# Norm 1's squares as diagonal blocks on TensorE, a far table laid out by lag column, and wider fillers, in a fused S4-and-MLP kernel

## The chip, the cores and the metric

The kernel runs on one core of one Trainium2 chip. The metric is the device time of one execution in microseconds (us), the median of several runs. A run is called slow when it lies over 1.5% above the fastest run of the same kernel; every comparison below is of fast runs unless it says otherwise. Within a trace, times count from the first instruction; the time of a run is about 1.7 us over its span.

TensorE is called PE in the views, its weight loads PEld, VectorE DVE, ScalarE ACT, GpSimd POOL; SP issues transfers. When this text speaks of a *row*, it means one instruction in TensorE's own stream: a weight load and its matmul are two rows, and a bare wait of its sequencer is one.

## The reference, cut to what matters

```python
def reference(A_u, ..., B_w1, B_b1, B_w2, B_b2):      # u: 2048 tokens x 512 channels
    # A: layernorm -> S4 convolution along the tokens (kernel K from A, B, C, dt) -> + u*Dskip
    K = jnp.einsum("dn,dnl,dn->dl", Cc, P, dB).real
    y = irfft(rfft(u_padded) * rfft(K_padded))[:L]
    h = x + A_ref(layernorm(x), ...)
    # B: layernorm -> MLP that mixes TOKENS: 2048 -> 1792 -> gelu -> 2048
    u = jnp.einsum("bsd,sf->bdf", layernorm(h), w1) + b1
    y = jnp.einsum("bdf,fs->bds", gelu(u), w2) + b2
    return h + y.transpose(0, 2, 1)
```

The kernel does the convolution in two ranges. Near lags go through small transforms of 128-token chunks; far lags through 32x32 *lag tiles* (`lag`) that multiply a *far table* G with the windowed means of earlier chunks, Mb. The first half of the chunks has its lag tiles early, the second half later.

## The kernel before: the parts that the change and the argument touch

Statistics of norm 1, on VectorE and ScalarE, two halves of eight 128-token chunks:

```python
def ln1(self, hf):
    for k in range(lo, hi):
        if k < hi - na:
            b.bn(self.st1[:, k, :], self.X[:, k, :])                       # VectorE, 512 wide
        else:                                                             # ScalarE, two passes
            b.act(self.junk[:, :], self.X[:, k], AF.Copy, accum_out=self.s1[:, 0, k:k + 1])
            b.act(self.cb[:, 0], self.X[:, k], AF.Square, accum_out=self.s1[:, 1, k:k + 1])
    ...                          # scales Fs, window weights WL, mean correction mb (PSUM bank 3)
def moments(self, hf):
    ...                          # ms = WL^T X + mb, in PSUM bank 3, copied out by ScalarE
def shifted(self, hf):
    # ms goes to HBM and comes back shifted, as Mb
```

The far table and the lag tiles:

```python
GB = (4, 2, 6)                    # first PSUM bank of each pair
def far(self):
    for i in range(0, NJ, 2):
        bb = GB[(i // 2) % len(GB)]
        for q in range(2):
            b.mm(self.bank(bb + q), self.tb("wi", (i + q) * P, P)[rows], self.kt[rows], pack=2)   # 512 columns
        ...                       # 1024-wide copies into G[p, x, i, s]
def lag(self, hf):
    for s in ...:
        for q in range(4):
            b.mm(self.ps[32*q:32*q+32, 32*s:32*s+32], Gv[:, q, s], Mv[:, q, s])   # 32x32 result tiles
```

The order of instructions on each engine isn't written by hand: a list scheduler in the program makes it at build time from priorities, dependencies and estimated costs. And it puts *fillers*, useless matmuls, where it expects TensorE to be idle.

```python
    self.near_kernel(); self.far(); self.lag(0)
    self.ln1(1); self.moments(1); self.shifted(1); self.spectrum(1)
    self.lag(1); self.rest(); self.mlp2()
    r.schedule(); r.emit_all()
```

## Time and profile before

| what | us |
|---|---|
| time, median of 3 runs (156.23 to 156.44) | 156.26 |
| span of the profiled run | 154.7 |
| big kernel table T complete | 35.17 |
| kt (short-lag values that the far table is made from) out of PSUM | 39.69 |
| first residual add, y0 | 50.11 |
| TensorE without gaps from | 57.45 |
| last addition starts | 152.34 |

Read it as a relay: tables on VectorE until 35, samples and far table until 45, lag tiles and convolution output until 57, and from there TensorE alone sets the end. The lines are in the prediction.

Two lines that the prediction did not show matter below: one of the waits (engine, line, what was waited for: us in total, times, longest), and one of the transfer queues, where *instruction* is the queue that brings instructions to the core (transfers, MB, share):

```profile
PE ps L499 <- issue: 0.4, 2, 0.2
```

```profile
q8 instruction: 12, 0.20, 0.5%
```

"issue" is idle time for which the profile shows no cause.

### The profile page before, as it was taken

How to read it: one execution, taken by the hardware profiler on the slowest of the kernel's cores; microseconds unless marked ns; L12 is line 12 of the kernel's file. 1: busy time of each engine (PE TensorE's matmuls, PEld its weight loads, DVE VectorE, ACT ScalarE, POOL GpSimd, SP SyncE). 2: the span in 40 equal slices, each digit the busy share in tenths (PEclk: the TensorE clock that was granted, in tenths of full speed). 3: DMA queues.
4: the chain of work that ended last, by engine and by line, in shares of the span. 5: the costliest groups of instructions: out<-in, count | busy, mean ns of one | idle time of the engine just before them, and what ended most of it. 6: DMA issues, size and time to landing. Idle time of an engine off the chain costs nothing.

```text
span 154.7 us, 3685 instructions
## 1 busy us (share of the span) xinstructions
PE 143.5 (93%) x1522; PEld 106.7 (69%) x1529; DVE 131.4 (85%) x308; ACT 78.2 (51%) x192; POOL 6.7 (4%) x11
## 2 busy tenths in 40 slices
PE   7849869989998889999999999999999999999993
PEld 3738753568565485545554788888888888888882
DVE  5099999998999998999999999957999994558663
ACT  4897999998997868614544832545320000000000
POOL 1590000000000000000000000000000000000000
PEclk9999999999999999999999999999999999999999
DMA  4899996266992508995590000000000101211123
GB/s 108 264 310 360 406 403 240 65 230 176 417 372 83 202 4 310 419 408 222 166 375 3 0 6 0 0 0 4 0 0 0 38 34 68 71 54 51 66 73 103
DMA packets 12351, 23.64 MB, mean 153 GB/s; under 512 B 1181, under 2 KB 8350, under 8 KB 12206
## 3 DMA queue, kind: packets, MB, share of 16 engines
q1 hardware_dynamic: 12190, 23.27, 41.8%
q8 instruction: 12, 0.20, 0.5%
q10 hardware_dynamic: 144, 0.13, 0.2%
q14 instruction: 5, 0.04, 0.1%
HBM read 21.17 MB, written 2.35 MB: 152 GB/s over the span
## 4 chain that ended last, share of the span: by engine, by line
PE 67%; DMA 14%; DVE 7%; SPq 5%; ACT 3%; issue 2%
PE ps L499 67%; DMA tab<-tables 8%; SPq L556 5%; DMA Mb<-ms_scratch 4%; DVE T L522 3%; DVE cmu L522 3%; DMA ms_scratch<-ms 2%; ACT G L506 1%; DVE ct L522 1%; ACT UF L506 1%; PE ps L784 1%; ACT ms L506 0%; ACT kf L506 0%; DVE X L536 0%; ACT mb L506 0%
## 5 line engine op out<-in xcount | busy, mean ns | idle before, releaser
L499 PE MATMUL ps<-H,W 128*128 128x512 bf16 (+1 forms) x180 | 32.5, 327 | 0.3 <-issue 0.2
L499 PEld LDWEIGHTS ps<-H,W 128*128 128x128 bf16 x184 | 17.7, 98 | 10.6 <-DVE H L532 0.2
L784 PE MATMUL ps<-idf 128*128 128x256 bf16 x162 | 22.0, 282 | 1.0 <-POOL idf L547 1.0
L499 PE MATMUL ps<-gT,W 128*128 128x256 bf16 x182 | 22.6, 273 | 0.0
L499 PEld LDWEIGHTS ps<-gT,W 128*128 128x128 bf16 x182 | 17.0, 98 | 3.0 <-DVE X L522 0.2
L784 PEld LDWEIGHTS ps<-idf 128*128 128x128 bf16 x162 | 15.6, 101 | 4.3 <-POOL idf L547 1.0
L522 DVE TENSOR_TENSOR W<-W 128x1024 bf16<-128x1024 bf16 (+1 forms) x23 | 14.9, 657 | 0.3 <-PE ps L499 0.2
L522 DVE TENSOR_TENSOR X<-ps,acc 128x256 bf16<-128x256 f32 x24 | 10.0, 422 | 5.5 <-PE ps L499 5.2
L499 PE MATMUL ps<-HT,W 128*128 128x256 bf16 x112 | 14.2, 273 | 0.0
L506 ACT ACTIVATE H<-X 128x512 bf16<-128x512 bf16 x16 | 10.0, 624 | 7.7 <-DVE X L536 7.7
L536 DVE SCALAR_TENSOR_TENSOR acc<-ps,b2T,X 128x256 f32<-128x256 f32 x24 | 11.1, 481 | 2.8 <-PE ps L499 2.2
L499 PEld LDWEIGHTS ps<-HT,W 128*128 128x128 bf16 x112 | 10.9, 98 | 1.4
L499 PE MATMUL ps<-TS,S 128*128 128x256 bf16 x84 | 11.6, 273 | 0.0
L499 PE MATMUL ps<-TS,W 128*128 128x256 bf16 x84 | 11.3, 273 | 0.0
L536 DVE SCALAR_TENSOR_TENSOR X<-ps,X 128x512 bf16<-128x512 f32 x16 | 10.6, 687 | 0.2 <-PE ps L499 0.2
L506 ACT ACTIVATE gT<-snap,b1T 128x256 bf16<-128x256 f32 x12 | 6.0, 505 | 9.1 <-DVE snap L522 9.1
L542 DVE BATCH_NORM_STATS2 st<-X 128x6 f32<-128x512 bf16 x12 | 7.4, 679 | 3.5 <-DMA X<-in_A_u_dram 3.5
L506 ACT ACTIVATE UF<-ps,ub 128x512 bf16<-128x512 f32 x16 | 10.2, 686 | 0.2 <-PE ps L499 0.2
L499 PEld LDWEIGHTS ps<-TS,S 128*128 128x128 bf16 x84 | 7.9, 98 | 1.4 <-DVE acc L536 0.4
L499 PEld LDWEIGHTS ps<-TS,W 128*128 128x128 bf16 x84 | 8.2, 98 | 1.0
L506 ACT ACTIVATE gT<-ps,b1T 128x512 bf16<-128x512 f32 (+1 forms) x10 | 5.4, 606 | 4.7 <-PE ps L499 4.7
L499 PEld LDWEIGHTS ps<-O,tab 128*128 128x128 bf16 x64 | 4.8, 98 | 3.9 <-DVE O L530 0.8
(127 smaller groups left out, 233.4 us busy)
## 6 DMA issues: line engine op xcount, KB each, us to landing
W<-in_B_w_dram SPq DMA_DIRECT2D x4, 1792.0 KB, 10.9
W<-in_B_w_dram SPq DMA_DIRECT2D x2, 2048.0 KB, 9.3
W<-in_B_w_dram SPq DMA_DIRECT2D x2, 1536.0 KB, 7.9
Mb<-ms_scratch SPq DMA_DIRECT2D x2, 1024.0 KB, 6.0
out_dram<-X SPq DMA_DIRECT2D x15, 128.0 KB, 1.7
tab<-tables SPq DMA_DIRECT2D x1, 1296.0 KB, 13.1
X<-in_A_u_dram SPq DMA_DIRECT2D x4, 256.0 KB, 4.7
X<-in_A_u_dram SPq DMA_DIRECT2D x2, 512.0 KB, 11.8
```

Of the source, the lines that this page charges most:

```text
L499: return self.r.add("pe", lambda e: e.matmul(out, lhsT=lhsT, rhs=rhs, start=start, stop=stop, skip_group_check=onto), [lhsT, rhs], [out], ...
L506: return self.r.add("act", lambda e: e.activation(out=out, in_=in_, func=func, bias=bias, scale=scale, accum_out=accum_out), [in_, bias, s ...
L522: return self.r.add(eng, lambda e: e.tensor_tensor(out=out, in0=a, in1=b, op=op), [a, b], [out], self._d(eng, nel(out), m), **k)
L536: return self.r.add(eng, lambda e: e.scalar_tensor_tensor(out=out, in0=a, scalar=s, in1=b, op0=op0, op1=op1, accum_out=accum_out), [a, s, ...
L542: return self.r.add("dve", lambda e: e.bn_stats(out=out, in_=a), [a], [out], 67 + nel(a) / 0.96, **k)
L556: return self.r.add(eng, lambda e: e.dma_start(out=out, in_=in_), [in_], [out], max(by / RATE.get(out.tensor.name.split("_")[0], 410) + 0. ...
L784: self.rec.hot = (hot, lambda e, bk: e.matmul(self.bank(bk, 0, 256), lhsT=hv[:, 0:P], rhs=hv[:, :], start=True, stop=True))
```

## The change

The intent: take norm 1's statistics off the crowded VectorE and ScalarE. X is loaded a second time, transposed, and TensorE squares it as 64-token diagonal blocks. The far table is made in blocks of four lag columns, so that the first lag tiles can start when half of it is copied, and is stored so that a tile's weight columns lie next to each other. The scheduler now counts lag tiles as four side by side (`slow` and `pack` change its cost estimates, not the instructions). One more pair of column blocks of MLP 1 uses the product with seven multiplications instead of eight. Fillers are 512 columns instead of 256 and start at 20.5 us instead of 8. The core of it, with cuts:

```diff
-GB = (4, 2, 6)
+GB = (4, 2, 6, 4)
-WARM = (8000.0, 48000.0)
+WARM = (27000.0, 48000.0)
+HOT = 20500.0
@@ loads
+        for h in range(2):
+            ld(17 + h, self.XT[:, h], self.x_in[0][L // 2 * h:L // 2 * h + L // 2], transpose=True)
+            ld(8 + h, self.X[:, 8 * h:8 * h + 8], xv[:, 8 * h:8 * h + 8])
@@ statistics (all of them before moments(0))
-                b.bn(self.st1[:, k, :], self.X[:, k, :])
+    def stats(self, hf):
+        for k in range(8):
+            for c in range(4):
+                for q in range(2):
+                    t = XT[:, c, P * k + 64 * q:P * k + 64 * q + 64]
+                    b.mm(self.bank(bk, 64*k, 64*k+64, 64*q, 64*q+64), t, t, start=c == 0, stop=c == 3, onto=True, pack=2)
+        ...   # 32 column sums per half; diagonal by a masked product and a reduction on VectorE
@@ far: 64 columns at a time, one lag column each
-                b.mm(self.bank(bb + q), self.tb("wi", (i + q) * P, P)[rows], self.kt[rows], pack=2)
+            for i in range(NJ):
+                for q in range(2):
+                    b.mm(self.bank(bb + q, 64*i, 64*i+64), self.tb("wi", i * P, P)[rows], kt[rows, c + q], pack=2)
@@ lag
-                    b.mm(self.ps[...], Gv[:, q, s], Mv[:, q, s])
+                    b.mm(self.ps[...], Gv[:, h, q, s - 16 * h], Mv[:, q, s], slow=8.5, pack=4)
@@ W1: two quarters before the tables and two after -> one after the first means, three after the second
-        for q in range(2):
-            ld(13 + q, self.W1[...], w1v[...])
+        self.w1q(*((1, 2, 3) if hf else (0,)))
@@ MLP 1: four pairs of column blocks -> five; fillers 256 -> 512 columns
```

## The prediction

> **What bounds the kernel now**

> I read the chain of waits first, then the busy table cut at the points where that chain changes engine, then the timelines of the five engines, and last the groups by shape. The chain, in order of time (start us, length us, what):

> ```profile
> 33.72 0.05 issue
> 33.76 3.49 PE ps L499 x126
> ...
> 40.21 1.94 ACT G L506 x2
> ...
> 44.22 0.70 ACT ms L506
> 44.91 0.02 issue
> 44.93 3.14 DMA ms_scratch<-ms
> 48.07 0.02 issue
> 48.09 6.31 DMA Mb<-ms_scratch
> 54.40 0.04 issue
> 54.44 2.85 PE ps L499 x114
> ...
> 81.83 70.49 PE ps L499 x621
> 152.32 0.03 issue
> 152.34 0.48 DVE X L536
> ```

> Up to 33.7 the chain is the VectorE making the kernel tables. Then TensorE samples them (x126), ScalarE copies the far table G, and the chain goes over to the second half of norm 1: its moments ms leave only at 44.2, go out to HBM and come back as Mb at 54.4. The second half of the lag products (x114 of 128) waits for that. From 57.4 on TensorE never stops. The busy time of each engine in those stretches (columns: PE, PEld, DVE, ACT, POOL, clock, DMA share, GB/s):

> ```profile
> 34.00:44.00 10.00, 9.72 (x225) 7.03 (x221) 9.26 (x21) 9.32 (x25) 0.00 (x0) 1.00 0.78 288
> 44.00:50.10 6.10, 5.42 (x144) 3.91 (x145) 5.82 (x9) 4.94 (x11) 0.00 (x0) 1.00 0.51 181
> 50.10:57.40 7.30, 6.36 (x157) 4.63 (x155) 7.30 (x18) 5.41 (x19) 0.00 (x0) 1.00 0.35 119
> 57.40:82.00 24.60, 24.39 (x148) 13.13 (x151) 23.60 (x61) 13.33 (x46) 0.00 (x0) 1.00 0.78 299
> 82.00:110.00 28.00, 28.00 (x239) 23.16 (x238) 24.52 (x64) 13.06 (x29) 0.00 (x0) 1.00 0.01 2
> 110.00:152.80 42.80, 42.30 (x384) 35.98 (x382) 32.34 (x76) 1.75 (x4) 0.00 (x0) 1.00 0.13 46
> ```

> The reader is to see three regimes. Before 50.1 the VectorE and ScalarE are both full and much of PE is filler. From 57.4 PE is full. And the VectorE is full too until 82, so what relieves PE there gives time only if the VectorE keeps up. A 256-column matmul goes at 92-94 per 10 us in the last stretches, 106.7 ns each, and twice that for 512 columns[...]. The gains must come from the first 57 us, or from fewer columns after it. The groups by shape concerned:

> ```profile
> L499 PEld LDWEIGHTS ps<-Mb,G 128*32 128x32 bf16 x256 | 5.5, 190 | 0.7 <-DMA Mb<-ms_scratch 0.4 <-issue 0.2
> L499 PEld LDWEIGHTS ps<-X,WL 128*32 128x32 bf16 x16 | 0.6, 96 | 1.2 <-DVE WL L522 0.4 <-ACT mb L506 0.3
> L542 DVE BATCH_NORM_STATS2 st<-X 128x6 f32<-128x512 bf16 x12 | 7.4, 679 | 3.5 <-DMA X<-in_A_u_dram 3.5
> L522 DVE TENSOR_TENSOR Fs<-tab,sm 128x1024 bf16<-128x1024 bf16 x2 | 2.4, 1222 | 0.2 <-DMA tab<-tables 0.2
> L506 ACT ACTIVATE G<-ps 128x1024 bf16<-128x1024 f32 x2 | 1.9, 1020 | 0.0
> ```

> The first two rows are loads of the same size, 128x32; the one from the far table takes twice as long.

> [...]In G now, neighbouring weight columns are 64 bytes apart; [...]190 ns against 96. [...]

> **The change part by part**

> (a) *Statistics of norm 1.* Out go 12 BN statistics on the VectorE (about 0.61 us apart, 7.3 us) and, on ScalarE, 4 copies and 4 squares with accumulators (0.62+0.19, overlapped about 0.7 each, 5.6 us). In come a transposed load of X (2 MB), 128 diagonal-block and 64 column-sum matmuls in free PE time, and two rounds of a 128x512 product from PSUM (0.69, as the residual add) and a reduction (about 0.6): 2.6 us of VectorE. More important than the sum is the place. Of the VectorE time removed 4.85 us lie at 7.5-12.4, ahead of the table work, and 2.5 us at 35.1-37.7, ahead of the second half's moments. The second half's statistics now come with the first's, near 20 us, so ms leaves at about 29 and Mb returns by about 41 rather than 54.4. The wait of 9.5 us (3.14+6.31) leaves the chain.

> DMA to this: raw parameters 0.8 MB, X twice 4 MB, tables 1.3 MB. At [...]the 330-400 GB/s that the trace shows for the rest (about 11 us), X is in by 22-25 us. Both W loads that ran before the tables move behind the moments. So the big table still lands near 21, as now (21.84), and 5.5 MB of W has until about 57.

> (b) *Fs of the first half to ScalarE* (eight 128x128, about 0.25 each, 2 us), saving 1.2 us of VectorE just where the table chain is (21.9-23.1). ScalarE has room for it, having lost 5.6 us. Two UF copies and one kf copy go to the VectorE (1.9 us), all eight lag copies of the first half to ScalarE (VectorE -1.3).

> (c) *Table chain, end at 35.17 now.* The VectorE ran 7.55-35.17 without a gap, 27.6 us. The statistics were 4.85 of it and Fs 1.2; the new ones add about 3. But ScalarE's table for Ln/Exp came at 18.7, and the T products and the scaling by rden cannot start before it. So I don't count 3 us but 2: that scaling starts at 20.5 rather than 23.0, and 0.5 is lost to the extra small operations. Samples end near 35.3.

> (d) *Far table.* 8 matmuls of 512 columns become 128 of 64. At the 27.7 ns of the sampling matmuls (3.49/126) that is 3.5 us rather than about 1.7. But copies are 512 wide and alternate between both engines (4 each at 0.6), and the first lag half needs only the first four. Now: kt done 39.7, first lag matmul 44.57, last 47.4, copies out 49.6. Then, from kt: 1.8 us of matmuls + 0.6 copy, lag products in the shadow of the other half, its end at 3.5+0.6 = 4.1, the second 64 lag products 0.8, copies 1.5. So 6.5 us after kt rather than 9.9: 3.4 us.

> (e) *Lag products.* 256 at 22.3 ns (2.86/128) = 5.7 us; with loads of half the length, about 12 ns, 3 us. 1.3 us of it lies in (d), 1.4 in the second half.

> (f) *MLP 1.* Six plain column blocks become four, and four block pairs five. Out: 2x16x213 = 6.8 us. In: 7x8x106.7 = 6.0 us. PE -0.85 us; VectorE +4 (four sums of 0.62, three adds of 0.35, and the first pair's sums which had been done before 50).

> *Sum.* The first residual add (y0) is at 50.11 now. 2 us (c) + 3.4 us (d, with e) puts it at 44.7; I take 45.5, since the VectorE must fit two kf products, G and UF copies into the same 8 us. Behind y0 PE now has 9.6 (other y matmuls: 16 chunks of 0.64 less one) + 2.85 (lag) + 20.5 + 23.9 + 41.8 (392x106.7) = 98.6 us of work in 102.7, so 4 us idle. Then it has 9.6 + 1.4 + 13.7 + 29.9 + 41.8 = 96.4. But the y stage then has only 24 us of PE work against 29 us of VectorE work: 16 residual adds 10.6, 16 norms 5.5, HT 5.5, two kf batches 4.7, pair sums 2.5. Products of the first pair that need no sums fill 1.7 of that. Idle rises from 4 to about 4.6: 101 us. Last addition: 45.5+101 = 146.5, against 152.8. The kernel's time is 3.4 over that (156.26-152.82), so 150.0 us.

> **The rivals**

> *The VectorE becomes the bound of the y stage.* For: 23.6 of 24.6 us at 57-82 already, and the PE relief of (f) is paid in VectorE work. Against: after 82 it has 14 us of slack to which sums can be put off. If it takes all of PE's gain: 152.5.

> *ScalarE's exponentials set the table chain.* For: it is 7.87 of 8 us busy at 16-24 and 8.00 at 24-32. Against: the accumulating passes leave. Then (c) gives nothing: 152.

> *The transposing load is slow or blocks the queue.* It stands ahead of X. [...]the second lag half waits again as now: 153-155.

> *All front gains hold and PE stays filled*: y0 at 44, no extra idle: 147.

> **Range and chances**

> 150.0, 4% below 156.26. The first two rivals give 152-152.5, the last 147, so 146.5 to 153 holds it 8 times in 10. 2% lies at 153.1: it takes a slow load, or two rivals together, to stay above that. Faster 0.85, same 0.12, slower 0.03.

> **What would show it**

> Right: no wait for Mb in the chain and both its loads landed before 43; the weight loads from G near 96 ns; y0 between 44 and 47; 280 pair matmuls in MLP 1; PE idle between y0 and 75, with the VectorE full, and none after. Wrong: y0 after 48, a wait for XT, X or W in the chain, PE gaps beyond 6 us after y0, or a clock row below full after 27 us.

The 0.6 us of a reduction in (a) is an estimate (0.68 in the changed kernel).

## The result, and the profile after

The changed kernel took **160.8 us** (160.71 to 161.58, 3 runs), where 150.0 was predicted. The ratio to before is 1.0302, 95% interval 1.0252 to 1.0353: slower. (Ratios are the mean time of one kernel's fast runs over that of the other's in the same rounds, so not quite the ratio of the medians.) The kernel before was run again in each later group, with medians of 156.9 to 157.4, so compare times of different groups by their ratios.

The chain of waits after the change, over the stretch that the prediction showed of before (start, length, what):

```profile
39.67 0.29 PE ps L507 x7
39.96 1.54 issue
41.50 0.34 PE ps L507 x9
...
43.94 1.83 issue
45.78 1.10 PE ps L507 x25
...
49.28 1.96 DMA ms_scratch<-ms
51.24 0.02 issue
51.26 5.15 DMA Mb<-ms_scratch
56.41 0.04 issue
56.45 1.14 PE ps L507 x109
57.60 2.92 issue
60.52 30.78 PE ps L507 x203
```

Two things stand out. The second half's means still leave late, at 49.28, even later than before. And there are three holes of 1.54, 1.83 and 2.92 us with no cause given, in the middle of groups of equal matmuls, where the next operand had long been there. The waits show the same; set them beside the 0.4 us of before:

```profile
PEld ps L507 <- issue: 11.8, 21, 3.0
PE ps L507 <- issue: 6.6, 4, 2.9
```

The busy table at three of the cuts of the prediction (length, PE, PEld, DVE, ACT, POOL, clock, DMA share, GB/s):

```profile
44.00:50.10 6.10, 4.32 (x89) 1.89 (x89) 5.13 (x5) 3.24 (x10) 0.00 (x0) 0.72 0.02 5
50.10:57.40 7.30, 6.60 (x166) 4.33 (x165) 5.48 (x18) 7.25 (x23) 0.00 (x0) 1.00 0.71 185
57.40:82.00 24.60, 21.68 (x153) 11.18 (x143) 20.39 (x53) 14.09 (x50) 0.00 (x0) 0.86 1.02 404
```

In the first row VectorE and ScalarE aren't crowded any more, as the change wanted, and TensorE has 1.8 us of idle time, and its clock is 0.72 of full where it was 1.00. In the last row it lost 2.9 us and has a clock of 0.86. The operations themselves came out as planned. By shape:

```profile
L507 PEld LDWEIGHTS ps<-Mb,G 128*32 128x32 bf16 x256 | 3.0, 97 | 7.0 <-issue 5.9 <-DMA Mb<-ms_scratch 1.0
L507 PE MATMUL ps<-kt,tab 64*128 64x64 bf16 x64 | 1.6, 190 | 1.8 <-issue 1.5 <-ACT G L514 0.2
```

The lag tiles' weight load is 97 ns where it was 190, and a run of 118 lag tiles takes 1.14 us, 9.7 ns each, where 128 took 2.85. But their idle time is 5.9 us of "issue". The queue of instructions has one transfer more:

```profile
q8 instruction: 13, 0.21, 0.6%
```

Each is 16384 bytes, which over 256 rows is 64 bytes a row. If TensorE's rows are numbered in order of their start, the three holes stand before rows 961, 1217 and 1729, which are 193 plus 3, 4 and 6 times 256. Before each resumption one of those transfers lands about 1.5 us earlier: 38.65 to 39.93 ahead of 41.50, 43.25 to 44.33 ahead of 45.78, 57.96 to 59.03 ahead of 60.52. This is the start of each row 193 + 256k, counted from the traces (a few records of matmuls are missing in some, so a number can be off by several):

```
row            705     961    1217    1473    1729
before        36.85   44.84   50.50   56.51   73.92
changed       34.04   41.50   45.78   54.50   60.52
hole before     -      1.54    1.83      -     2.92
```

In the kernel before, 256 rows never take less than 5.6 us there. In the changed kernel, with the holes taken off, the three blocks that end in one ran in 5.9, 2.4 and 3.1 us (41.50 - 34.04 - 1.54, and so on), because many operations have become smaller or faster and there are more of them: 3326 rows in all against 3064 (16 and 13 of them bare waits).

### The profile page after: what moved, and what is told of

Same layout as the page of the kernel before. It is cut to its first block, busy times and chain, and to the rows that moved or that the text cites. A ratio compares the mean times of both kernels' runs of the same rounds, so it can differ in the third digit from the quotient of the medians.

```text
span 159.0 us, 3930 instructions
## 1 busy us (share of the span) xinstructions
PE 137.4 (86%) x1655; PEld 100.8 (63%) x1655; DVE 128.7 (81%) x300; ACT 76.4 (48%) x190; POOL 6.7 (4%) x11
## 4 chain that ended last, share of the span: by engine, by line
PE 60%; DMA 15%; DVE 11%; SPq 6%; issue 5%; ACT 1%
PE ps L507 59%; DMA W<-in_B_w_dram 6%; DMA XT<-in_A_u_dram 5%; SPq L564 3%; DMA Mb<-ms_scratch 3%; SPq L557 3%; DVE cmu L530 3%; DVE S L530 2%; DVE W L530 2%; DVE T L530 1%; PE ps L792 1%; DMA ms_scratch<-ms 1%; DVE ct L530 1%; DVE gd L530 0%; ACT ms L514 0%
## 5 line engine op out<-in xcount | busy, mean ns | idle before, releaser
L507 PE MATMUL ps<-H,W 128*128 128x256 bf16 (+1 forms) x168 | 28.4, 317 | 0.0
L507 PE MATMUL ps<-gT,W 128*128 128x256 bf16 x182 | 23.6, 273 | 0.0
L507 PEld LDWEIGHTS ps<-H,W 128*128 128x128 bf16 x168 | 16.5, 99 | 9.1 <-issue 1.3
L507 PE MATMUL ps<-HT,W 128*128 128x256 bf16 x128 | 16.6, 273 | 0.1
L507 PEld LDWEIGHTS ps<-HT,W 128*128 128x128 bf16 x128 | 12.4, 98 | 1.8 <-DVE snap L530 0.4
L514 ACT ACTIVATE snap<-ps 128x256 f32<-128x256 f32 x15 | 5.7, 384 | 9.7 <-PE ps L507 9.5
L514 ACT ACTIVATE gT<-snap,b1T 128x256 bf16<-128x256 f32 x15 | 7.3, 503 | 5.7 <-DVE snap L530 5.7
L507 PE MATMUL ps<-Mb,G 128*32 128x32 bf16 x256 | 4.2, 188 | 5.5 <-issue 4.8
L540 DVE TENSOR_SCALAR H<-X,sm 128x512 bf16<-128x512 bf16 x16 | 5.9, 407 | 2.8 <-ACT sm L514 2.8
L507 PEld LDWEIGHTS ps<-Mb,G 128*32 128x32 bf16 x256 | 3.0, 97 | 7.0 <-issue 5.9
L507 PE MATMUL ps<-X,Fs 128*128 128x512 bf16 x16 | 7.2, 448 | 0.3 <-issue 0.3
```

The costliest lines, as they stand in the source:

```text
L507: return self.r.add("pe", lambda e: e.matmul(out, lhsT=lhsT, rhs=rhs, start=start, stop=stop, skip_group_check=onto), [lhsT, rhs], [out], ...
L514: return self.r.add("act", lambda e: e.activation(out=out, in_=in_, func=func, bias=bias, scale=scale, accum_out=accum_out), [in_, bias, s ...
L540: f = lambda e: e.tensor_scalar(out=out, in0=a, scalar1=s1, scalar2=s2, op0=op0, op1=op1)
```

## The experiments

All eighteen runs gave correct results. "Useless matmuls" are 16 columns wide, read a constant tile, write to a PSUM bank that is free there and are read by nobody.

### First group: move the cuts, undo parts

`e1_pad128` inserts 64 useless matmuls, 128 rows, half a block, into free TensorE time at 5.7 and 15 us, and holds the order of everything else.

```diff
+DUMMY = [('c:pe', 32), ('gm1:pe', 32)]          # section ahead of which, how many
         r.schedule()
+        for sec, n in DUMMY:
+            ...  pe.insert(at, matmul(bank 7, 0:16) on the constant tile)
```

> The changed kernel with 64 useless matmuls of 16 columns (128 TensorE rows) put where TensorE is idle early (32 before the BC products, 32 before the second diagonal-block group); every engine's order is otherwise held. Theory F (TensorE gets its instructions in blocks of 256, and a block is refilled only after the one before has been used up, in 3.5 us with the DMA idle and 6 to 7.5 us beside bulk loads): the stops stay at the same row numbers of the TensorE stream (961, 1217, 1473, 1729), so they move to instructions 128 rows earlier; the stop of 2.9 us in the second lag half goes, because its block is asked for before the W loads start, and the time falls by 2 to 5 us to 156-159. Theory M (changing the tile shape of the array, or a hidden wait of that instruction, makes the stop): the stops stay before the same instructions and the time stays at 160.8 or rises by up to 1.

It took 156.3 us (156.08 to 157.58), ratio 0.996, interval 0.9904 to 1.0015. More work, 4.5 us less time. The hole in the second lag half is gone, all 128 tiles run in one piece, and one hole is left, at another tile of the first half:

```profile
45.28 0.36 PE L508 MATMUL ps<-Mb,G 128*32 128x32 bf16 x25 [2.64 <-issue]
57.38 1.22 PE L508 MATMUL ps<-Mb,G 128*32 128x32 bf16 x128 [0.74 <-DMA Mb<-ms_scratch]
```

Rival M falls: the tiles are the same and in the same order.

`e1_w1_late` issues the first quarter of W1 after the second half's means, so that it does not run beside the first holes.

```diff
-        self.w1q(*((1, 2, 3) if hf else (0,)))
+        self.w1q(*((0, 1, 2, 3) if hf else ()))
```

> The changed kernel with the first quarter of W1 issued after the second half's moments, beside the other three quarters, instead of at 32.6 us; every compute engine's order is held. Theory F with the DMA as part of it: the instruction transfer that starts at 38.65 now starts by about 35-36.5, and the first stop (1.54 us at row 961) falls to under 0.5 us; the second stop (row 1217) stays at 1.3-2 us because it comes of the burst of short matmuls, and the third stays or grows. Time 158.5-160.5. If bulk loads don't matter to the instruction transfer (theory M, or F from the burst alone), the first stop stays at about 1.5 us and the time at 160.8.

159.16 us, ratio 1.013 (1.0086 to 1.0173). The holes were 0.85, 1.30 and 2.92 us. A partial miss: the instruction transfer still began at 38.6, while the Mb loads were still in flight. The edit becomes useful below, once the cut lies elsewhere.

`e1_far_whole` makes the far table by 8 matmuls of 512 columns again, 112 rows fewer, with the new layout kept.

```diff
-            for i in range(NJ):
-                for q in range(2):
-                    b.mm(self.bank(bb + q, 64*i, 64*i+64), self.tb("wi", i * P, P)[rows], kt[rows, c + q], pack=2)
+            for q in range(2):
+                b.mm(self.bank(bb + q), self.tb("wi", (i + q) * P, P)[rows], self.kt[rows], pack=2)
```

> The changed kernel with the far table made by 8 matmuls of 512 columns as before the change, copied by pairs into the new order of G; this takes 240 rows from the TensorE stream in the stretch of the stops and lets the scheduler order the rest anew. Theory F: with 496 rows fewer in that burst, at most one of the first two stops is left and the stops together fall from 6.3 us to under 4 us; time 156-159, although the first lag half must now wait for the whole table. Theory M: the lag products, with their tile shapes, are all still there, so the two stops in them (1.8 and 2.9 us) stay and the time is 160-161.

173.95 us, ratio 1.1037 (1.0966 to 1.1109). Of the three holes only one was left (1.74 us, at row 959). But the time says nothing about the far table: the scheduler, given other costs, made another order throughout, and in MLP 1 ScalarE's copies waited 22.3 us for TensorE in place of 9.5. An edit that changes what the scheduler sees changes everything after it, so most later runs hold the order.

`e1_mom_early` gives the second half's moments the highest priority.

```diff
-PRIO: 'wl1:dve': 36.2, 'wl1:pe': 20.5, 'mb1:pe': 9.5, 'mom1:pe': 14.8, 'mb1:act': 13.6, 'mom1:act': 27.1
+PRIO: 'wl1:dve': 5,    'wl1:pe': 1,    'mb1:pe': 1,   'mom1:pe': 1,    'mb1:act': 1,    'mom1:act': 1
```

> The changed kernel with higher priority for the second half's window weights, means and moments (six priorities), so that they go before the sampling matmuls. If my prediction's step (a) failed only through the order (the second half's moments behind the table work): the second ms leaves before 36 us rather than at 49.3, both Mb halves land before 44, and no wait for Mb is left at 56.4. The gain in time is then 2-4 us if the wait for Mb bounds; under theory F the second lag half then joins the burst and stops of about 1.5-3 us per 256 rows stay, so the time falls only to 158-160.

162.32 us, ratio 1.0317 (1.0262 to 1.0372), and the means left at 51.04, no earlier. So it was not just the order. The program shows why: with `GB = (4, 2, 6, 4)` the far table's second pair takes PSUM banks 2 and 3, the moments use bank 3, and the far table is written before them. They must wait until that pair is copied out. The kernel before has the same banks (its three entries are taken in turn) and the same program order, so this is not new.

### Second group: controls

`e2_pad256` inserts twice as many, 256 rows, a whole block: `DUMMY = [('c:pe', 64), ('gm1:pe', 64)]`.

> The changed kernel with 128 useless 16-column matmuls put into free TensorE time before the tables (64 and 64), which moves every later instruction of the queue on by 256 rows, a whole block, where the run with half as many moved them by half a block. Theory F (TensorE gets its instructions in blocks of 256 rows, at fixed row numbers): the blocks cut the work at the very instructions where they cut the changed kernel, so the stops come back before the same tiles (about 1.5, 1.8 and 2.9 us) and the time is 160 to 162 us. Rival (useless matmuls help in another way, for instance by keeping TensorE's clock up or by delaying something): the gain of the run with half as many stays or grows, 155 to 157 us.

161.43 us, ratio 1.0305 (1.023 to 1.0379): the gain is gone. And the holes are back at the same tiles. In the timeline of TensorE (start, length, what, and in brackets the idle time before it), the changed kernel, then this run:

```profile
41.50 0.78 PE L507 MATMUL ps<-kt,tab 64*128 64x64 bf16 x41 [1.54 <-issue]
45.78 0.39 PE L507 MATMUL ps<-Mb,G 128*32 128x32 bf16 x27 [1.83 <-issue]
60.52 0.27 PE L507 MATMUL ps<-Mb,G 128*32 128x32 bf16 x10 [2.92 <-issue]
```

```profile
43.47 0.78 PE L508 MATMUL ps<-kt,tab 64*128 64x64 bf16 x41 [3.10 <-issue]
...
47.19 0.38 PE L508 MATMUL ps<-Mb,G 128*32 128x32 bf16 x27 [1.04 <-issue]
...
62.18 0.27 PE L508 MATMUL ps<-Mb,G 128*32 128x32 bf16 x10 [3.06 <-issue]
```

Both leave 41 far matmuls, 27 lag tiles and 10 lag tiles behind the cut. A shift by half a block moved the cuts, a whole block put them back.

`e2_pad128_hot` is the first pad with 7 of its matmuls 512 columns wide, to keep TensorE busy from 16 us on, as theory C asks.

```diff
+            emit = filler of 512 columns if sec == 'gm1:pe' and j % 5 == 0 else useless matmul of 16 columns
```

> The run with 64 useless matmuls again, with the same number of rows at the same places, but 7 of the second 32 are 512-column matmuls, so TensorE is busy for some 3 us more at 15 to 19 us, just ahead of the moments, where it is idle in the changed kernel. Theory C (the cold start that the removed 512-column fillers of before had hidden costs time): TensorE is at full clock from about 20 us, the tables and the first residual add come up to 1 us earlier, and the time falls below that of the run with 64 small ones by 0.5 to 1.5 us. Rival (until 35 us ScalarE and VectorE set the pace, the clock there costs nothing): within 0.4 us of that run, 156 to 156.6 us.

156.28 us, ratio 0.998 (0.9897 to 1.0063): the same as without. The six fillers after 20 us took 1.46 us instead of 2.72, 0.24 us each instead of 0.45, so the slow start was gone, and nothing came of it. Theory C falls for the cold start up to 25 us; from 24.8 to 35.0 the clock was at half in this run (in the changed kernel from 31.46 to 34.88), so that stretch was not tested.

`e2_mom_first` moves three calls, and `e2_mom_first_pad128` adds the pad.

```diff
+        self.ln1(1); self.moments(1); self.shifted(1)
         self.far(); self.lag(0)
-        self.ln1(1); self.moments(1); self.shifted(1)
```

> The changed kernel with the second half's moments written before the far table in the program, so that they no longer wait for the far table's second pair of banks to be copied out; nothing else. If that bank is what held them (step (a) of the prediction failed by the bank, not by the order): the second half's means are out before 40 us (49.28 in the changed kernel), Mb lands before 50, and the wait of the second lag half for Mb is gone. Theory F says the stops stay somewhere, since about as many rows run as closely as before, so the time falls by 1 to 3 us only, 158 to 160. Rival (the late means set the time, the stops only fill a wait that is there anyway): 154 to 156 us.

> Both edits: the second half's moments before the far table, and 64 useless small matmuls ahead of the tables. Theory F with the bank: the means leave early and the blocks are cut elsewhere; if the new cuts fall as well as they did in the run with the matmuls alone, 153 to 156 us; if they fall in the middle of the lag work, 157 to 160 with stops of 1.5 to 3 us at row numbers 961, 1217, 1473 or 1729, and at no others.

172.5 us (ratio 1.0998, 1.0903 to 1.1094) and 173.06 us (1.1032, 1.0961 to 1.1103): both expectations missed, and for the reason of `e1_far_whole`; ScalarE's copies in MLP 1 waited 23.0 us. One thing can be read: the means left at 44.19 instead of 49.28, so the bank was part of it. The time was no test.

### Third group: provoke the holes in the kernel before, and hold the order

`e3_before_rows512` and `e3_before_fill24` take the kernel *before* and put useless work ahead of its first lag tile: 256 small matmuls (512 rows), or 24 of 512 columns (48 rows).

```diff
+        for _ in range(256):   pe.insert(at, matmul(bank 0, 0:16))     # e3_before_rows512
+        for _ in range(24):    pe.insert(at, matmul(bank 0, 0:512))    # e3_before_fill24
```

> The kernel before, not the changed one, with 256 useless 16-column matmuls (512 rows of TensorE's queue, two whole blocks) put right before its first lag tile, at about 44.6 us, where it has no stop. At some 20 ns each, as its own 128 lag tiles take there, they are 5 us of work. Theory F: rows are used up faster than blocks of 256 arrive, so the useless rows themselves are cut by waits marked issue, two of 1 to 3 us at row numbers 1217 and 1473, and the kernel loses the 5 us plus 2 to 5 us: 163 to 167 us. Rival M (stops belong to the changed kernel's own tiles or waits, not to the number of rows): no such stops, the loss is the work alone, at most 5 us: 159 to 162 us.

> Control of the run with 512 useless rows: at the same place in the kernel before, 24 fillers of 512 columns (217 ns each, 5.2 us of work, but only 48 rows). Theory F: no stop, the loss is at most the 5.2 us of work: 159 to 162 us, and 2 to 5 us less than the run with 512 rows. Rival M: the same as that run within 1 us.

165.96 us (ratio 1.0547, 1.0476 to 1.0618) and 162.85 us (1.0311, 1.0222 to 1.0401). The timeline of the first, then of the second:

```profile
44.73 3.70 PE L754 MATMUL ps<-idf 128*128 128x16 bf16 x142
48.89 3.09 PE L754 MATMUL ps<-idf 128*128 128x16 bf16 x114 [0.47 <-issue]
51.91 0.52 PE L499 MATMUL ps<-Mb,G 128*32 128x32 bf16 x14
53.99 2.57 PE L499 MATMUL ps<-Mb,G 128*32 128x32 bf16 x114 [1.56 <-issue]
```

```profile
45.78 5.34 PE L754 MATMUL ps<-idf 128*128 128x512 bf16 x24
51.05 2.90 PE L499 MATMUL ps<-Mb,G 128*32 128x32 bf16 x128
```

The holes appear in the kernel before, at rows 1215 and 1471 by the count, one of them inside useless matmuls that wait for nothing and one inside its own lag tiles. They are smaller than expected (2.0 us together, not 2 to 6), as the useless matmuls took 26 ns each rather than 20 and so left the fetch more time. The control lost 5.5 us by the medians, about its 5.3 us of work, and has no hole; its time was 0.85 us over the range given.

`e3_mom_held` is `e2_mom_first` with every engine's order taken from the changed kernel, and only the moments' matmuls and two copies moved ahead of the far table. `e3_mom_held_pad128` adds the pad.

```diff
+ORDER = {...}      # the changed kernel's order of each engine, written out
+   pe:  wl1, mb1, mom1 moved ahead of G0;   act: mb1, mom1 moved ahead of G0
```

> The changed kernel with every engine's order of instructions held as it is, except that the second half's moments (X with WL, nm with tab, and the rank-one products, with their two ScalarE copies) stand just ahead of the far table, which the bank allows as the program now has them before the far table. If the bank and the order were what held them, the means are out at 41 to 43 us instead of 49.28 and the second lag half no longer waits for Mb (56.41 in the changed kernel). Theory F: the stops stay (the count of rows is the same), so the time falls by 0 to 1.5 us: 159.5 to 161 us. Rival (late means are what costs the 4.5 us): 155.5 to 157 us.

> The same, and the 64 useless small matmuls ahead of the tables. Theory F: the cut at row 1729 stays out of the second lag half, and as that half no longer waits for Mb either, the time is at or below the run with the useless matmuls alone (156.3): 154.5 to 156.5 us. Rival (one hidden wait takes the other's place, gain nothing): 156.3 within 0.4 us or more.

159.41 us (ratio 1.0136, 1.0065 to 1.0207) and 158.32 us (0.999, 0.9882 to 1.0097; two of its four runs, the profiled one among them, were slow, so its fast runs are 158.17 and 156.07). In the first the means left at 46.23, later than expected because a hole of 2.31 us fell inside the moments, and the wait for Mb was gone while the hole of 2.87 us in the second lag half was not. By the ratios that is 1.6% under the changed kernel (1.0136 against 1.0302), though the first two holes moved as well, so it isn't the means alone; the larger part of the loss stays. The second is inconclusive: with two fast runs 2 us apart it shows neither a gain nor none.

### Where the microseconds of the third hole go

In the kernels that hold the changed kernel's order, the same instruction can be found in each by counting rows from the end. Times between such rows, worked out from the traces:

```
rows from the end        1600 -> 1500     1500 -> last     clock, 60.5 to 72 us
changed kernel               11.14            90.36             0.78
e2_pad256                    11.49            90.31             0.70
e1_pad128                     7.16            90.31             1.00
e2_pad128_hot                 6.42            90.31             1.00
```

Everything behind row 1500 from the end, 57% of the kernel, takes the same time in all four. The whole gain of the pad is made in a hundred rows around the third hole: 11.14 against 7.16 or 6.42 us. The hole itself is 2.92 us. The rest fits the clock: in the changed kernel it is at half for 6.8 us, from within the hole on (58.8 to 65.6), and 512-column matmuls there start 0.43 us apart, where they start 0.22 us apart at full clock.

### Fourth group: take the holes away

If what is left above 150 is also holes, a version with none should come near it. With the pad, the only hole left was the one in the first lag half. In `e1_pad128` row 961 starts at 38.22, and the transfer for the next block begins only at 42.88, with a W1 quarter in flight between. So now the W1 edit again, with the pad (`e4_pad128_w1`), then all edits (`e4_mom_pad128_w1`), with 48 useless matmuls (`e4_mom_pad96_w1`), and with the wide ones (`e4_mom_pad128_w1_hot`).

```diff
+   sp:  first W1 quarter moved behind the second half's means                      # all four
+   pe, act: moments ahead of the far table, order held                             # the last three
+DUMMY = [('c:pe', 32), ('gm1:pe', 32)]        # 24 and 24 in e4_mom_pad96_w1
```

> The changed kernel in its own order, with the 64 useless small matmuls ahead of the tables and the first W1 quarter issued after the second half's means instead of beside the Mb loads. Theory F: the block after row 1217 is asked for at some 38 us and then has only the Mb loads beside it, which end at 38.6, so it is there by 41 to 42 us, before it is needed, and the first lag half has no stop over 0.7 us; 153.5 to 155.5 us, against 156.3 with the useless matmuls alone. Rival (the chain of tables and means is what is left): the stop goes or shrinks and the time stays at 156 within 0.5 us.

> All three: the moments ahead of the far table with the order held, 64 useless matmuls, the first W1 quarter late. Theory F with the clock: no stop over 0.7 us between 34 and 62 us, no half-clock stretch there but what a wait for data leaves, and no wait for Mb: 151.5 to 154.5 us, faster than the kernel before. Rival (chain): 155.5 to 157 us.

> The same with 48 useless matmuls instead of 64, which moves every cut 32 rows later in the work. By theory F the cut at row 1729 still falls inside the second lag half with its block asked for 6 to 7 us before, so nothing changes there, and the cut at row 1217 comes 32 rows later, some 0.6 us more time for its block: within 1 us of the run with 64, 151.5 to 155 us.

> The run with all three, and 7 of the second 32 useless matmuls are 512 columns wide, so that TensorE is at full clock before the moments and tables of 20 to 36 us. In the earlier pair of runs this took 0.02 us off the median and 1.4 us off the profiled span. If the cold start costs time once the stops are gone: 0.5 to 1.5 us under the run with all three; if not, the same within 0.4 us.

| run | median us (runs) | ratio to before | 95% interval |
|---|---|---|---|
| e4_pad128_w1 | 155.54 (5) | 0.9922 | 0.9877 to 0.9967 |
| e4_mom_pad128_w1 | 154.42 (6) | 0.9843 | 0.9812 to 0.9873 |
| e4_mom_pad96_w1 | 154.79 (4) | 0.986 | 0.9811 to 0.9908 |
| e4_mom_pad128_w1_hot | 154.0 (6) | 0.9827 | 0.9794 to 0.9861 |

The first was 0.04 us over its range, the second and third within theirs; the last, 0.42 us under the second, fell between its two. In `e4_pad128_w1` row 961 starts at 37.72 and the transfer begins at 38.46, 0.7 us later in place of 4.7, and no hole over 0.4 us without a named cause is left. Between these two runs only the W1 quarter differs, so that bulk loads delay the fetch is shown for this place. All four beat both kernels, by 0.8 to 1.7% against before (their intervals lie below 1, but none reaches 2%) and, dividing the ratios by 1.0302, by 3.7 to 4.6% against the changed one. The wide useless matmuls take 0.4 us off the median and 0.24 us off the mean, with intervals that overlap almost wholly: no gain from the warmer start is shown. In this last version the last stretch before the MLP reads

```profile
44.00:50.10 6.10, 4.84 (x163) 2.94 (x158) 6.03 (x7) 5.55 (x15) 0.00 (x0) 1.00 0.46 105
50.10:57.40 7.30, 5.31 (x166) 3.67 (x166) 7.30 (x22) 7.15 (x24) 0.00 (x0) 1.00 1.03 383
57.40:82.00 24.60, 24.27 (x160) 13.90 (x160) 24.29 (x66) 16.07 (x50) 0.00 (x0) 1.00 1.00 396
```

with full clock and x163 where the changed kernel had x89 in the same 6.1 us. VectorE and ScalarE are full from 50 to 57, while TensorE has 2 us of idle time there; they look like the bound now.

### Fifth group: is the useless work needed, and does it help the kernel before too?

`e5_mom_w1` is the best version without useless matmuls; `e5_before_pad128` is the kernel before with 64 of them, 32 near 5.5 us and 32 ahead of its first fillers.

```diff
-DUMMY = [('c:pe', 32), ('gm1:pe', 32)]       # e5_mom_w1: none
+DUMMY = [('c:pe', 32), ('hot:pe', 32)]       # e5_before_pad128, in the kernel before
```

> The kernel before with 64 useless 16-column matmuls (128 rows) in early TensorE time, 32 near 5.5 us and 32 ahead of its first fillers. It has no stop to lose, so by theory F there is nothing to gain: within 1 us of the kernel before, no faster than 0.5 us under it. Rival (useless matmuls help any kernel here): 1.5 us or more under the kernel before.

> The best version without its useless matmuls: the moments ahead of the far table and the first W1 quarter late, row numbers as in the changed kernel. Theory F: the stop at row 1729 inside the second lag half is back (2 to 3 us, with a half-clock stretch behind it), so 156.5 to 159.5 us, 2.5 to 5 us over the version with them. Rival (the useless matmuls did nothing once the other two edits are in): 154.0 to 154.8 us.

`e5_mom_w1`: 158.41 us, ratio 1.0137 (1.0085 to 1.0189). The hole in the second lag half is back, before its last 11 tiles:

```profile
59.03 0.26 PE L509 MATMUL ps<-Mb,G 128*32 128x32 bf16 x11 [2.48 <-issue]
```

So some 2 us of useless matmuls in free time are worth 4 us here. `e5_before_pad128`: 155.54 us, ratio 0.9929 (0.9885 to 0.9972). I had said no more than 0.5 us under; it is 1.3 us under by the medians, 0.7% by the ratio. The kernel before has no hole to lose in either trace, so this small gain has another cause that I didn't find. In the two profiled runs 0.38 us of it is there when T is complete (34.79 against 35.18), and 0.36 us comes after y0. It does mean that of the best version's 1.7% only about 1% is more than useless work gives by itself.

## Why the prediction was wrong, point by point

The prediction's steps beside the changed kernel and beside one run without holes (`e4_pad128_w1`; its profiled run, at 154.1 us, was the fastest of its five):

| step | predicted | changed | without holes |
|---|---|---|---|
| T complete | 33.2 | 35.1 | 35.2 |
| kt out of PSUM | 37.7 | 39.9 | 40.5 |
| kt to first residual add y0 | 7.8 | 11.9 | 7.7 |
| y0 | 45.5 | 51.8 | 48.2 |
| y0 to last addition | 101 | 104.8 | 101.9 |
| last addition | 146.5 | 156.6 | 150.05 |
| kt to last addition | 108.8 | 116.7 | 109.6 |

**What failed was the sum's silent term.** Steps (d) and (e) and the last part of the sum added up the work, and the work was right to about 1.5 us: from kt to the last addition 108.8 us were predicted, and the four runs without holes take 109.6 to 110.2 us. The changed kernel takes 116.7. (That kt to y0 agrees to 0.1 us in the table is luck of that one run: the other three have 9.9 to 10.0 us before y0 and 100.1 to 100.4 after it.) None of the terms asked whether TensorE's instructions would be there. By these traces the holes, with the half-clock stretches behind them, cost 6.5 to 7.2 us of the 10.8 us by which the time was missed; a little of it is not theirs, as these runs carry the W1 edit and three of them that of the moments. A block's end cost 0.5 to 3.2 us (0.47 in `e3_before_rows512`, 3.20 in `e1_mom_early`) where TensorE would have run 256 rows faster than the next block came. The rows weren't counted: (a) added 384 rows of statistics and the far table 112 (it has 64 matmuls, where (d) put 128), while (e) made 512 rows of lag tiles twice as fast. A small misreading of its lines: a 256-column matmul takes 109 ns from start to start in the trace before (median of 600 from 82 us on), not 106.7; the count of 92 to 94 in 10 us takes in those that the window cuts. Over the last 392 matmuls that is 0.9 us.

**Step (c), 2 us from the table chain: nothing came.** This was the second rival, in part. T was complete at 35.1 (35.17 before). At the front VectorE waited 6.09 us for ScalarE and began with the tables at 10.18, where it had begun at 12.31, so only 2.1 of the 4.85 us taken away came free. This is the first table operation, before and after:

```profile
12.31 0.41 DVE L522 TENSOR_TENSOR m<-EX,CX 128x512 bf16<-128x512 bf16 x1
```

```profile
10.18 0.88 DVE L530 TENSOR_TENSOR m<-EX,CX 128x512 bf16<-128x512 bf16 x1 [6.09 <-ACT CX L514]
```

Inside the chain the new statistics then took 2.4 us (two products, two reductions), and where Fs of the first half had gone, Fs of the second came in, 1.2 us. The scaling by rden (reciprocals that ScalarE makes) started at 22.8 (23.0 before, 20.5 predicted); rden was ready at 22.1. So ScalarE set the start, and VectorE, which from 10.18 on had one gap of 0.39 us, the rest. 2 us of the error.

**Step (a), means out at 29 and Mb back at 41: wrong.** They left at 49.28 and Mb came at 56.41. The step reckoned with when the operands are there. It overlooked a PSUM bank: the far table's second pair takes bank 3, which the moments need, as it did before the change. And the second half of X, which they also need, landed only at 28.19. Higher priority didn't help; writing the moments first and moving them in the held order did (43.13 in the best version, by its trace, still 14 us after the predicted 29; no run had the moments earlier). The loss by itself was small, 0.70 us of wait in the changed kernel, as the hole stands just behind it.

**The transposed load.** The packets of the two transfers of 1 MB ran from 6.98 to 11.33 and from 12.23 to 16.75 us, 241 and 232 GB/s. They landed at 11.81 and 18.76, X followed at 21.79 and 28.19, where 22 to 25 was predicted for all of it, and the big table came at 25.03, not near 21. The second transposed half stands in the chain of waits (from 10.92, 7.84 us long), which was one of the prediction's signs of being wrong. VectorE lost 0.39 us by it, so the third rival explains little of the time.

**Right:** the lag tiles' weight load (97 ns, 96 predicted), five pairs in MLP 1, TensorE's total work falling (busy 137.4 us, 143.5 before), VectorE full behind y0. The list of what would show it wrong held the right signs: y0 after 48, a wait for XT and one for W in the chain, and a clock row below full after 27 us. TensorE's gaps after y0 came to 3.8 us, not beyond its 6.

**The clock.** The prediction expected slow matmuls at the start alone. Here the clock fell to half at 45.12 and 58.77, 1.2 us after the second and the third hole began, for 3.4 and 6.8 us. The hole of 1.54 us had no such fall behind it: full clock lasted for 3.6 us after its end. Nor was there a hole before every fall: the clock was at half from 31.46 to 34.88 with 0.9 us of scattered idle time and no hole from 28.0 to there, and in `e3_before_rows512` from 50.72, where TensorE had run 16-column matmuls since 44.73 with one idle stretch, of 0.47 us. That the half-clock stretch after 58.77 goes where the third hole goes is shown (from 60.5 to 72 us the clock is 1.00 in `e1_pad128`, 0.78 in the changed kernel); what makes the clock fall is not.

**Open:** the last addition of the best version starts at 150.6 in its trace, 4.1 us after the predicted 146.5. Of that 1.8 us is there when T is complete, that is step (c); 1.0 us comes between T and kt, where TensorE's clock is still at half until 35.3; and 1.2 us comes behind kt, where ScalarE and VectorE are full from 50 to 57. No run took these apart. And 0.7% in the kernel before with useless matmuls has no explanation.

## What to carry to other kernels

Count instructions as well as time: where a stretch becomes a dense run of tiny matmuls, see how long 256 of TensorE's rows take. Where the next block set the time here, it took 3.7 to 4.5 us, and 4.8 to 8.8 us beside bulk loads; if the rows take less, a hole at the block's end is to be looked for, unless bulk loads stay away and the cut falls elsewhere. An unexplained "issue" wait in the middle of equal instructions is a sign of it, and shifting everything by half a block with useless instructions in free time is a cheap test. And where a scheduler makes the order, hold the order when testing one edit, or the run tests the scheduler.

## The fetch and the transposed load, as measured here

- TensorE stopped at the ends of blocks that came too soon, for 0.5 to 3.2 us. In the changed kernel each transfer of a block between 34 and 65 us began 1.1 to 4.6 us after a block had started (34.04 and 38.65, 41.50 and 43.25, 45.78 and 46.88, 54.50 and 57.96, 60.52 and 64.39), as though there were room for the block in use and one more; that is a reading of these times, no run tested it. From the start of one block to that of the next, where a hole shows the fetch to be the limit, took 3.7 to 4.5 us where other transfers filled less than half of the transfer engines' time (3.72 in `e1_w1_late`, 41.34 to 45.06; 4.28 in the changed kernel), and 4.8 to 8.8 us beside bulk loads (6.02 and 7.46 in the changed kernel). In one place bulk loads were shown to delay the fetch: with a W1 quarter in flight it took 4.7 us until it began (`e1_pad128`), without one 0.7 (`e4_pad128_w1`).
- The packets of two transposing loads of 1 MB came at 241 and 232 GB/s in the changed kernel. Each held its issuing queue for 4.2 to 4.4 us, and they landed 6.4 and 7.8 us after their issue.
